# Two first weight pieces issued by ScalarE, and a last product that starts fresh in two PSUM banks, in an FNet and ReGLU mix on one core

## The chip, the cores and the metric

The kernel runs on 1 core of one Trainium2 chip. The metric is the device time of one execution in microseconds. The kernel before ran three times: 781.6, 779.49 and 779.66 us, median 779.66. One further execution was profiled; every row shown below from the kernel before is from it.

## The reference

```python
def a_ref(x, seq_re, seq_im, hid_re, hid_im):
    a = einsum("bsd,ed->bse", x, hid_re)
    b = einsum("bsd,ed->bse", x, hid_im)
    return einsum("ts,bse->bte", seq_re, a) - einsum("ts,bse->bte", seq_im, b)

def b_ref(x, W_gate, W_up, W_down):
    gate = einsum("bsd,df->bsf", x, W_gate)
    up   = einsum("bsd,df->bsf", x, W_up)
    gate = gate * (gate > 0)
    return einsum("bsf,fd->bsd", gate * up, W_down)

g = sigmoid((x * gate_w).sum(-1, keepdims=True))
out = g * a_ref(x, ...) + (1 - g) * b_ref(x, ...)
```

`x` is 1 x 2048 x 512 in fp32, the hidden size of the second branch is 1792, the matrices of the first are the cosines and sines of a Fourier transform over the hidden and the sequence dimension.

## The kernel before

**How the work is tiled.** Every matrix product is cut into 2 x 2 blocks and done as seven block products on sums of blocks (m = 1 to 7) instead of eight. Each fp32 operand is split in two parts that TensorE takes: `hi`, a rounded copy made by a ScalarE `copy` (CAST in the profile), and `lo`, what is left, made by a VectorE subtraction. One tile product is then three matmuls, left lo with right hi, left hi with right lo, left hi with right hi (`PARTS`, L365). A step of 128 x 512 outputs is one matmul row of the profile; a matmul on 256 columns is half of one.

**What sets the order.** No engine call is issued where it stands in the code. `op(key, f)` records a step, `pe(n, f)` records n matmuls and moves the clock of keys on, and `Plan.order` (L191) walks through all steps with a cost model (a matmul, a landing of a DMA, an issue per queue) and picks, for VectorE, ScalarE, SyncE and GpSimd, which step comes next; TensorE keeps the order of the code. `Step.run` (L122 to L126) then issues everything, so that all rows of the profile carry line L126, and names of tiles tell them apart. The order on each engine is fixed when the program is built: an engine that waits for one step holds all that stand behind it.

**Queues.** `load` (L356) is a DMA issued by SyncE (SP), which loads and writes most plain tiles. `store` and `accumulate` are issued by GpSimd. Before the change ScalarE issues no DMA.

**The start.** `warm_up` (L1230) sets `gs` to zero on VectorE and puts 18 matmuls of 256 columns on a constant into PSUM while the first loads are on their way. The first block product, m = 1, is done for two weight blocks, `ws[0]` and `ws[1]` (called w0 and w1 below; their raw tiles are `wr0`, two halves n of the columns and two halves k of the contraction each). TensorE's order is six matmuls on w0 with k half 0, six on w0 with k half 1, six and six on w1, then 24 matmuls of m = 2 (which need `x21`, the tile `x021`, and the column halves n = 1 of w0 and w1), then m = 5 and so on. `x11` (tile `x011`) comes in two halves, w0 in two quarters n = 0, k = 0 and k = 1, and the rest in larger pieces (L1254 to L1263). ScalarE casts each piece, VectorE takes the rest of it.

**The end.** `Joint` (L1067) is the last of the Fourier rounds: for y in `ORDER_Z` = (1, 5, 6, 3, 7, 2, 4), m in (0, 1) and hh in (0, 1) it records `product` (L1156), six matmuls each with left sides `self.w` and a right side `jc` that `right` (L1138) loads, casts on ScalarE (`jch`) and completes on VectorE (`jcl`). `evac` (L1167) combines the PSUM banks into the outputs `jo0` and `jo1`: with `last=True` it multiplies by the gate (`gg`), adds what the output already held (`jv0`, `jv1`) and writes by SP. `lead` gives how many keys ahead of their product the loads and the splits are planned. In the last call (L1388) the order is rearranged so that both products of y = 2 and y = 4 for m = 0 stand ahead of those for m = 1, and both products of y = 4, m = 1 are done in two column halves: ScalarE copies the second half of the bank of y = 4 into another bank, so that the first half can be finished and evacuated while the second is multiplied. The accumulations go on from m = 0 in those banks.

**The stage ahead of the end.** A `Shorter` round writes its outputs as `z`: VectorE adds two PSUM banks and a copy, then multiplies by the gate. Its last right sides are `cl`.

Of the kernel before, what the change touches and what calls it, by code (L numbers as in the profile page):

```python
# [14 lines left out]
P = 128  # L15
# [113 lines left out]
class Plan:  # L129
# [3 lines left out]

    MATMUL, WAIT, LANDING, COLD = 0.22667, 0.035, 2.5, 2.3

    ISSUE = {"sync": 0.5, "scalar": 0.5, "gpsimd": 0.9}

    REST = 60
# [52 lines left out]
    def order(self):  # L191
# [12 lines left out]
        while any(todo.values()):  # L204
            best = None
            for e, queue in todo.items():
                found = None
                near = queue[:1] if e == "tensor" or not queue else [*queue[:48], min(queue, key=turn.get)]
                for s in near:
                    if any(x.start is None for x in s.after):  # L210
                        continue
                    t = max(free[e], now)
                    for x in s.after:
                        t = max(t, x.end + (0 if x.engine == e else self.WAIT + 0.16 * (x.engine == "tensor")))
                    if e != "tensor":
                        t = max(t, (s.key - self.AHEAD[e]) * self.MATMUL + late)
                    new = {r.base for r in (*s.writes, *s.reads) if r.base.kind == "unit" and r.base not in begun}
                    if new:
                        short = live + bisect_left(ahead, turn[s]) + len(new) - UNITS
                        if short > 0:  # L220
                            if len(ends) < short:
                                continue
                            t = max(t, ends[short - 1])
                    if found is None or t < found[0] - 0.12:
                        found = t, s, new
                if found and (best is None or found[0] < best[0]):
                    best = found
            if best is None:
                raise ValueError(f"no way on at {len(done)}: {[(e, q[0].key, q[0].name) for e, q in todo.items() if q]}")
            t, s, new = best  # L230
            now = t
            while ends and ends[0] <= t:
                ends.pop(0)
                live -= 1
            live += len(new)
            for b in new:
                ahead.remove(min(turn[x] for x in b.uses))
            begun |= new
            todo[s.engine].remove(s)
            s.start = t  # L240
            if s.name == "dma_start":
                free[s.engine] = t + self.ISSUE[s.engine]
                line = max(line, free[s.engine]) + s.work * (self.COLD if 2.3 < t < 2.9 else 1)
                s.end = line + self.LANDING + (2.0 if "accum_op" in s.k else 0)
            else:
                s.end, free[s.engine] = t + s.work, t + s.hold
            if s.engine == "tensor" and s.key >= 0:
                late = max(late, t - s.key * self.MATMUL - 6 * self.MATMUL)
            for b in {r.base for r in (*s.writes, *s.reads) if r.base.kind == "unit"}:
                left[b] -= 1  # L250
                if not left[b]:
                    ends.append(max(x.end for x in b.uses))
                    ends.sort()
            done.append(s)
# [24 lines left out]
def kernel(ctx: ExitStack, tc, xP, xG, wgu, wd, cr, ci, wri, gw, out):  # L279
# [36 lines left out]

    gs = Buf(plan, "gs", [2, 32], kind="fixed", tile=small.tile([P, 2, 32], F32, name="gs"))

    gx = Buf(plan, "gx", [2, 32], kind="fixed", tile=small.tile([P, 2, 32], F32, name="gx"))

    def buf(name, shape=(2, N), dtype=F32):
# [80 lines left out]
    class Weights:  # L402
# [7 lines left out]
            self.d = buf("wd", [2, 2, 2, P], F32R)  # L410
            self.b = [[buf(f"wb{h}{x}", [2, 2, 2, P], F32R) for x in "hl"] for h in range(2)]

        def load(self, h, n=slice(0, 2), k=slice(0, 2)):
            load(self.raw[h][:, n, k], wgu[self.c, h, :, n, k])

        def a_hi(self, n=slice(0, 2), k=slice(0, 2)):
            E().scalar.copy(self.a[0][:, n, k], self.raw[0][:, n, k])
# [649 lines left out]
    class Joint:  # L1067
# [5 lines left out]
        def __init__(self, ms, banks, x=2, raw=None, last=False, lead=(0, 0), own=()):  # L1073
# [9 lines left out]
                op(base - 40, lambda: load(self.v[0].all, od[x - 2, :, 0:2]))  # L1083
                op(base + 20, lambda: load(self.v[1].all, od[x, :, 1]))
            order = [(y, m) for y in ORDER_Z for m in ms]
            if last:
                order[-4:] = [(y, m) for m in ms for y in ORDER_Z[-2:]]
            for n, (y, m) in enumerate(order):
                for hh in range(2):
                    self.right(m, y, hh, base + 12 * n + 6 * hh, made.get((m, hh)))  # L1090
            for y, m in order:
                for hh in range(2):
                    pe(6, self.product, m, y, hh)
                if m == ms[-1]:
                    self.evac(y, plan.now)
                elif last and y == 4:
                    op(plan.now, lambda: E().scalar.copy(self.half(1), self.bank(4, HALVES[1])))

        def lefts(self, m, base, raw, wide):
            if raw is None:  # L1100
# [37 lines left out]
        def right(self, m, x, hh, key, made):  # L1138
# [5 lines left out]

            if not made:
                op(key - self.READ - self.lead[0], read)
            op(key - self.HI - self.lead[1], lambda: E().scalar.copy(hi.all, raw.all))
            op(key - self.LO - self.lead[1], lambda: E().vector.tensor_sub(lo.all, raw.all, f32(hi.all)))

        def bank(self, x, cols=slice(0, N)):  # L1150
            return ps8[:, PAIRS[self.banks[BANK[x] in "yt"]].n + (BANK[x] in "mt"), cols]

        def half(self, n):
            return ps8[:, PAIRS["y"].n, HALVES[1]] if n else self.bank(4, HALVES[0])

        def product(self, m, x, hh):  # L1156
            l, c = self.w[m, x], self.c[m, x, hh]
            begin, end = m == self.ms[0] and hh == 0, m == self.ms[-1] and hh == 1
            halves = self.v and x == 4 and m == self.ms[-1]
            for cols in HALVES if halves else (slice(0, N),):  # L1160
                ps = self.half(HALVES.index(cols)) if halves else self.bank(x)
                for i in range(2):
                    for n, (a, b) in enumerate(PARTS):
                        mm(ps, l[a][:, 2 * hh + i], c[b][:, i, cols], start=x in FIRST and begin and i == n == 0,
                           stop=x not in (1, 5, 6, 7) and end and i == 1 and n == 2)

        def evac(self, x, key):  # L1167
            X, Y, M, T = (self.bank(k) for k in (1, 6, 5, 4))
# [25 lines left out]
            elif v:  # L1194
                for n, cols in enumerate(HALVES):
                    out, t = o[0][:, 1, cols], self.half(n)
                    op(key, lambda out=out, t=t, cols=cols: e.vector.tensor_mul(out, t, g[:, 0, cols]))
                    op(key, lambda out=out, cols=cols: combine(out, out, v[0][:, 1, cols], 1))
                    op(key, lambda out=out, cols=cols: load(od[self.x - 2, :, 1, cols], out))
            else:  # L1200
                op(key, lambda: e.vector.tensor_mul(o[0][:, 1], T, g[:, 0]))
# [27 lines left out]

    def warm_up():  # L1230
        E().vector.memset(gs.all, 0.0)
        for n in range(WARM):
            half = slice(n % 2 * (N // 2), (n % 2 + 1) * (N // 2))
            mm(ps8[:, (2, 3, 6, 7)[n // 2 % 4], half], ones[:, :P], ones, start=n in (0, 2, 4, 6), stop=True)
# [19 lines left out]
    for k in halves:  # L1254
        op(-99, x_load(0, "11", k))
        op(-99, ws[0].load, 0, halves[0], k)
    op(-99, ws[1].load, 0, halves[0])
    op(-99, x_load(0, "21"))
    for w in ws:
        op(-99, w.load, 0, halves[1])  # L1260
    op(-98, x_load(0, "12"))
    for w in ws:
        op(-98, w.load, 1)  # L1263
# [121 lines left out]
    Shorter(lb, 1, 1)  # L1385
    opened.resume(plan.now - 10)
    Shorter(lb, 1, 0)
    Joint((0, 1), "xm", last=True, lead=(80, 30))  # L1388

    plan.run(nc, unit)  # L1390

# [51 lines left out]
```

## Time and profile before

| what | us |
| --- | --- |
| median of three runs | 779.66 |
| the profiled execution | 779.72 |
| its span, first to last instruction | 777.9 |
| VectorE busy (736 instructions) | 665.5 |
| ScalarE busy (499 instructions) | 425.9 |
| GpSimd busy (178 instructions) | 121.5 |

The profiled execution lies 0.06 us above the median, and 1.82 us of it lie outside the span. The rows give an engine's time, the instructions of one kind, and in brackets what an engine waited for before them. PEld are TensorE's weight loads, which run beside its matmuls; a bracket on a PEld row is a wait of TensorE. SPq is the issuing of a DMA on SyncE's queue.

### The profile page before, as it was taken

The page shows a single profiled execution, that of the slowest core. Times are in us where ns is not written, and L with a number is a line of the kernel's source. Part 1 is how long each engine was busy: PE and PEld are TensorE (multiplying, and loading weights), DVE is VectorE, ACT ScalarE, POOL GpSimd, SP SyncE. Part 2 cuts the span into 40 slices and gives each one's busy share as a digit, 9 for nine tenths or more (in the row PEclk, how much of TensorE's full clock was granted, in tenths as well). Part 3 has the DMA queues.
Part 4 walks back from the last instruction along what each step waited for, and adds up shares of the span by engine and source line. Part 5 has one row for each costly group of instructions (what it writes and reads, how often), then busy time and mean ns, then how long its engine had stood idle before and what let it go on. Part 6 is the DMA issues. An engine that isn't in the chain of part 4 may idle for free.

```text
span 777.9 us, 9558 instructions
## 1 busy us (share of the span) xinstructions
PE 772.3 (99%) x3414; PEld 638.3 (82%) x3414; DVE 665.5 (86%) x736; ACT 425.9 (55%) x499; POOL 121.5 (16%) x178
## 2 busy tenths in 40 slices
PE   9999999999999999999999999999999999999997
PEld 7888888888888888888888888888888888888886
DVE  6999766766778685999996999998699899699898
ACT  6666444434455443566653667547644755345791
POOL 0021333332222332211000000030002011001000
PEclk9999999999999999999999999999999999999999
DMA  9246497999897999775369789989989997999982
GB/s 324 82 150 163 162 267 227 314 300 251 229 322 281 337 408 405 276 279 187 94 208 380 267 262 389 373 172 266 310 294 206 356 306 167 284 250 305 388 278 55
DMA packets 60255, 205.65 MB, mean 264 GB/s; under 512 B 7152, under 2 KB 7664, under 8 KB 60208
## 3 DMA queue, kind: packets, MB, share of 16 engines
q1 hardware_dynamic: 37264, 122.72, 43.5%
q0 software_dynamic: 22944, 82.32, 39.2%
q8 instruction: 27, 0.44, 0.2%
q14 instruction: 20, 0.16, 0.1%
HBM read 155.45 MB, written 74.73 MB: 296 GB/s over the span
## 4 chain that ended last, share of the span: by engine, by line
PE 98%; DMA 1%; SPq 0%; ACT 0%; DVE 0%; issue 0%; DVEq 0%
PE ps L126 98%; DMA x<-xP 1%; SPq L126 0%; DVE jo L126 0%; ACT xh L126 0%; ACT wah L126 0%; DVEq L126 0%
## 5 line engine op out<-in xcount | busy, mean ns | idle before, releaser
L126 PE MATMUL ps<-ch,ll 128*128 128x512 f32 x516 | 200.7, 389 | 0.0
L126 PE MATMUL ps<-cl,lh 128*128 128x512 f32 x516 | 200.7, 389 | 0.0
L126 PE MATMUL ps<-ch,lh 128*128 128x512 f32 x516 | 200.7, 389 | 0.0
L126 ACT CAST ch<-r 128x1024 fp32r<-128x1024 f32 x80 | 82.1, 1054 | 74.1 <-DVE r L126 64.6
L126 PEld LDWEIGHTS ps<-ch,ll 128*128 128x128 f32 x516 | 96.9, 188 | 20.1
L126 PEld LDWEIGHTS ps<-cl,lh 128*128 128x128 f32 x516 | 96.9, 188 | 20.1
L126 PEld LDWEIGHTS ps<-ch,lh 128*128 128x128 f32 x516 | 96.9, 188 | 20.0
L126 DVE TENSOR_TENSOR cl<-r,ch 128x1024 fp32r<-128x1024 f32 x80 | 95.6, 1221 | 7.7 <-ACT ch L126 6.1
L126 ACT CAST ch<-hr 128x1024 fp32r<-128x1024 f32 (+1 forms) x56 | 51.8, 945 | 43.5 <-DVE hr L126 21.2
L126 DVE TENSOR_TENSOR jcl<-jc,jch 128x1024 fp32r<-128x1024 f32 x56 | 65.6, 1222 | 7.8 <-issue 3.9
L126 ACT COPY s<-ps 128x1024 f32<-128x1024 f32 (+1 forms) x52 | 46.0, 884 | 47.6 <-PE ps L126 46.3
L126 ACT CAST jch<-jc 128x1024 fp32r<-128x1024 f32 x56 | 56.2, 1052 | 16.1 <-PE ps L126 14.0
L126 DVE TENSOR_TENSOR cl<-hr,ch 128x1024 fp32r<-128x1024 f32 (+1 forms) x56 | 60.1, 1087 | 5.1 <-ACT lh L126 2.7
L126 ACT ACTIVATE ps<-ps 128x512 f32<-128x512 f32 (+1 forms) x42 | 33.0, 785 | 55.0 <-PE ps L126 52.6
L126 POOL DMA_DIRECT2D out<-z x20 | 14.6, 729 | 297.3 <-DVE z L126 290.0
L126 DVE TENSOR_TENSOR r<-r,r 128x1024 f32<-128x1024 f32 x48 | 57.6, 1220 | 0.2
L126 DVE TENSOR_TENSOR u<-ps,s 128x1024 f32<-128x1024 f32 x28 | 34.1, 1221 | 13.4 <-PE ps L126 8.8
L126 POOL DMA_DIRECT2D hd<-h x35 | 23.0, 662 | 136.9 <-DVE h L126 125.6
L126 PE MATMUL ps<-xh,wb0l 128*128 128x512 f32 x112 | 43.8, 391 | 0.0
L126 PE MATMUL ps<-xh,wb0h 128*128 128x512 f32 x112 | 43.6, 389 | 0.0
L126 PE MATMUL ps<-xl,wb0h 128*128 128x512 f32 x112 | 43.6, 389 | 0.0
L126 PE MATMUL ps<-xh,wb1l 128*128 128x512 f32 x112 | 43.6, 389 | 0.0
(161 smaller groups left out, 1536.1 us busy)
## 6 DMA issues: line engine op xcount, KB each, us to landing
hr<-hd SPq DMA_DIRECT2D x33, 512.0 KB, 5.1
jc<-td SPq DMA_DIRECT2D x32, 512.0 KB, 8.1
td<-ci POOLq DMA_DIRECT2D x24, 512.0 KB, 10.1
r<-cr SPq DMA_DIRECT2D x24, 512.0 KB, 9.5
r<-ci SPq DMA_DIRECT2D x24, 512.0 KB, 8.5
out<-z POOLq DMA_DIRECT2D x20, 512.0 KB, 7.2
l<-ad SPq DMA_DIRECT2D x18, 512.0 KB, 8.7
wr<-wgu SPq DMA_DIRECT2D x16, 512.0 KB, 8.3
```

Source lines behind the costliest of these rows:

```text
L126: getattr(getattr(nc, self.engine), self.name)(*map(ap, self.a), **{k: ap(x) for k, x in self.k.items()})
```

## The change

At the start, the first piece of w1 (both k halves of its columns n = 0) and the second piece of w0 (its columns n = 1) are issued by ScalarE's queue, and no longer by SP's. A copy of `gs` into a new small tile `first` is put on ScalarE ahead of them, and the planner holds a DMA of ScalarE until 1.4 in its own time. At the end, the rearranged order is dropped; only the very last product (y = 4, last m, hh = 1) is in column halves; each half starts fresh in a bank of its own; its right side is multiplied by the gate beforehand; a new step `rest` multiplies what the bank of y = 4 holds by the gate and adds `jv0`; and the evacuation of a half is one addition. The lead of the last call changes from (80, 30) to (70, 44).

```diff
+    TABLE = 1.4
 ...
+                    if e == "scalar" and s.name == "dma_start":
+                        t = max(t, self.TABLE)
 ...
+    first = Buf(plan, "first", [32], kind="fixed", tile=small.tile([P, 32], F32, name="first"))
 ...
-        def load(self, h, n=slice(0, 2), k=slice(0, 2)):
-            load(self.raw[h][:, n, k], wgu[self.c, h, :, n, k])
+        def load(self, h, n=slice(0, 2), k=slice(0, 2), queue=None):
+            (queue or load)(self.raw[h][:, n, k], wgu[self.c, h, :, n, k])
 ...
-            if last:
-                order[-4:] = [(y, m) for m in ms for y in ORDER_Z[-2:]]
 ...
                 for hh in range(2):
+                    if self.fresh(m, y, hh):
+                        op(plan.now, self.rest)
                     pe(6, self.product, m, y, hh)
                 if m == ms[-1]:
                     self.evac(y, plan.now)
-                elif last and y == 4:
-                    op(plan.now, lambda: E().scalar.copy(self.half(1), self.bank(4, HALVES[1])))
 ...
+            if self.fresh(m, x, hh):
+                op(key - self.HI - self.lead[1] - 8, lambda: E().vector.tensor_mul(raw.all, raw.all, self.gate(0).to_broadcast([P, 2, N])))
 ...
+        def fresh(self, m, x, hh):
+            return self.v is not None and x == 4 and m == self.ms[-1] and hh == 1
+
         def half(self, n):
-            return ps8[:, PAIRS["y"].n, HALVES[1]] if n else self.bank(4, HALVES[0])
+            return ps8[:, PAIRS["y"].n + n, HALVES[n]]
 ...
-            halves = self.v and x == 4 and m == self.ms[-1]
+            halves = self.fresh(m, x, hh)
 ...
-                        mm(ps, l[a][:, 2 * hh + i], c[b][:, i, cols], start=x in FIRST and begin and i == n == 0,
+                        mm(ps, l[a][:, 2 * hh + i], c[b][:, i, cols], start=(x in FIRST and begin or halves) and i == n == 0,
 ...
+        def rest(self):
+            out = self.o[0][:, 1]
+            E().vector.tensor_mul(out, self.bank(4), self.g[:, 0])
+            combine(out, out, self.v[0][:, 1], 1)
 ...
-                    op(key, lambda out=out, t=t, cols=cols: e.vector.tensor_mul(out, t, g[:, 0, cols]))
-                    op(key, lambda out=out, cols=cols: combine(out, out, v[0][:, 1, cols], 1))
+                    op(key, lambda out=out, t=t: combine(out, out, t, 1))
 ...
         E().vector.memset(gs.all, 0.0)
+        E().scalar.copy(first[:], gs[:, 0])
 ...
-    op(-99, ws[1].load, 0, halves[0])
+    op(-99, ws[1].load, 0, halves[0], whole, plan.scalar.dma_start)
     op(-99, x_load(0, "21"))
-    for w in ws:
-        op(-99, w.load, 0, halves[1])
+    op(-99, ws[0].load, 0, halves[1], whole, plan.scalar.dma_start)
+    op(-99, ws[1].load, 0, halves[1])
 ...
-    Joint((0, 1), "xm", last=True, lead=(80, 30))
+    Joint((0, 1), "xm", last=True, lead=(70, 44))
```

The order of the instructions moves at three places. The first is ScalarE's at the start of the program; `wr0_84` is w0's raw tile before the change and `wr0_101` is w1's. Before:

```order
L126 ACT_TABLE_LOAD
L126 CAST wah_109<-wr0_84 128x256 x2
L126 CAST wah_131<-wr0_101 128x256 x2
L126 COPY ps_75<-ps_75 128x1024
L126 CAST xh2_155<-x021_103 128x512 x2
L126 CAST wah_109<-wr0_84 128x512
L126 COPY ps_75<-ps_75 128x1024
L126 CAST wah_131<-wr0_101 128x512
```

Now, where `wr0_86` is w0's and `wr0_95` w1's:

```order
L126 ACT_TABLE_LOAD
L126 COPY first_74<-gs_73 128x32
L126 DMA wr0_95<-wgu 128x512
L126 DMA wr0_86<-wgu 128x512
L126 CAST wah_115<-wr0_86 128x256
L126 CAST wah_131<-wr0_95 128x256
L126 CAST wah_115<-wr0_86 128x256
L126 CAST wah_131<-wr0_95 128x256
L126 CAST wah_115<-wr0_86 128x512
L126 COPY ps_76<-ps_76 128x1024
L126 CAST xh2_156<-x021_106 128x512 x2
L126 CAST wah_131<-wr0_95 128x512
```

Besides the copy and the two DMAs, the first cast of w1 now stands ahead of the second cast of w0, and the cast of w0's columns n = 1 and the copy of the bank ahead of the casts of `x21`. VectorE's subtractions of the same pieces change places in the same way. On SP the two pieces are gone: `x21` is now the fifth DMA and w1's second piece the sixth, where they were the sixth and the eighth.

The second place is VectorE's order around the last but one `z` before the end. Before:

```order
L126 TENSOR_TENSOR jll_5796<-js5_5691,jlh_5777 128x1024
L126 TENSOR_TENSOR jcl_5818<-jc_5624,jch_5790 128x1024
L126 TENSOR_TENSOR cl4_5828<-r11_5375,ch4_5807 128x1024
L126 TENSOR_TENSOR jcl_5843<-jc_5636,jch_5824 128x1024
L126 TENSOR_TENSOR z12_5855<-ps_75,s6_5679 128x1024
L126 TENSOR_TENSOR z12_5855<-z12_5855,gg_5510 128x1024
L126 TENSOR_TENSOR jll_5874<-js5_5716,jlh_5813 128x1024
L126 TENSOR_TENSOR jcl_5882<-jc_5648,jch_5841 128x1024
L126 TENSOR_TENSOR cl4_5893<-r11_5404,ch4_5859 128x1024
```

Now:

```order
L126 TENSOR_TENSOR jcl_5810<-jc_5654,jch_5796 128x1024
L126 TENSOR_TENSOR jll_5821<-js5_5716,jlh_5781 128x1024
L126 TENSOR_TENSOR jcl_5830<-jc_5664,jch_5813 128x1024
L126 TENSOR_TENSOR cl4_5848<-r11_5377,ch4_5824 128x1024
L126 TENSOR_TENSOR z12_5860<-ps_76,s6_5675 128x1024
L126 TENSOR_TENSOR z12_5860<-z12_5860,gg_5513 128x1024
L126 TENSOR_TENSOR jcl_5879<-jc_5680,jch_5832 128x1024
L126 TENSOR_TENSOR jll_5887<-js6_5692,jlh_5840 128x1024
L126 TENSOR_TENSOR jcl_5898<-jc_5694,jch_5866 128x1024
L126 TENSOR_TENSOR cl4_5910<-r11_5406,ch4_5875 128x1024
```

Two steps of the last call, one `jll` and one `jcl`, have moved from behind this `z` to ahead of it, and three steps instead of two stand between its gating and `cl4`, the last right side of the round.

The third place is the end of VectorE's order. Before:

```order
L126 TENSOR_TENSOR jcl_6208<-jc_5982,jch_6180 128x1024
L126 TENSOR_TENSOR jo1_6192<-ps_75,js_6052 128x512
L126 TENSOR_TENSOR jo1_6192<-jo1_6192,gg_5990 128x512
L126 TENSOR_TENSOR jo1_6192<-jo1_6192,jv1_6012 128x512
L126 TENSOR_TENSOR jo0_6231<-ps_75,gg_5990 128x512
L126 TENSOR_TENSOR jo0_6231<-jo0_6231,jv0_5870 128x512
L126 TENSOR_TENSOR jo0_6231<-ps_75,gg_5990 128x256
L126 TENSOR_TENSOR jo0_6231<-jo0_6231,jv0_5870 128x256
L126 TENSOR_TENSOR jo0_6231<-ps_75,gg_5990 128x256
L126 TENSOR_TENSOR jo0_6231<-jo0_6231,jv0_5870 128x256
```

Now:

```order
L126 TENSOR_TENSOR jc_6018<-jc_6018,gg_6007 128x1024
L126 TENSOR_TENSOR jo1_6172<-ps_76,js_6072 128x512
L126 TENSOR_TENSOR jo1_6172<-jo1_6172,gg_6007 128x512
L126 TENSOR_TENSOR jcl_6213<-jc_6018,jch_6203 128x1024
L126 TENSOR_TENSOR jo1_6172<-jo1_6172,jv1_6025 128x512
L126 TENSOR_TENSOR jo0_6224<-ps_76,gg_6007 128x512
L126 TENSOR_TENSOR jo0_6224<-jo0_6224,jv0_5892 128x512
L126 TENSOR_TENSOR jo0_6224<-ps_76,gg_6007 128x512
L126 TENSOR_TENSOR jo0_6224<-jo0_6224,jv0_5892 128x512
L126 TENSOR_TENSOR jo0_6224<-jo0_6224,ps_76 128x256 x2
```

The gating of the last right side is new; the gating and adding of y = 4 are now one pair of 512 columns ahead of the last product; behind the last product one addition for each half is left. On TensorE, twelve of the 24 matmuls of 256 columns became six of 512. ScalarE's copy of the bank's second half is gone.

## The prediction

> **What bounds the kernel now.** I read the head of the page first, then the chain of waits in order of time.
>
> ```profile
> span 777.9 us, 9558 instructions
> ...
> 3.07 6.43 DMA x<-xP
> ...
> 11.23 761.70 PE ps L126 x3366
> ...
> 774.28 0.42 DVE jo L126
> ```
>
> TensorE (PE) owns 761.70 of 777.9 us in one unbroken piece: 3366 matmuls at 761.70 / 3366 = 0.2263 us each. Nothing that moves on VectorE (DVE), ScalarE (ACT) or the queues inside that piece can help; it can only hurt by making PE wait. What can be won lies at the two ends: ahead of 11.23, where the chain goes through the landing of `x21`, and behind the last matmul. The profiled execution took 779.72 us, 0.06 above the median of 779.66, and all sums below are made against 779.72. A difference under 0.3% (2.34 us) is about what a measurement of this kernel can tell from no change.
>
> **The start as it is.** The timeline of SP's queue, ACT and PE, each with start, duration and in brackets what it waited for:
>
> ```profile
> 0.74 0.38 SPq L126 DMA_DIRECT2D x<-xP  x1
> ...
> 2.12 0.91 SPq L126 DMA_DIRECT2D wr<-wgu  x2
> ...
> 0.74 1.28 ACT L126 ACT_TABLE_LOAD   x1 [0.74 <-PEq L1436]
> ...
> 5.50 0.41 ACT L126 CAST wah<-wr 128x256 fp32r<-128x256 f32 x1 [0.84 <-DMA wr<-wgu]
> ...
> 7.94 1.00 ACT L126 COPY ps<-ps 128x1024 f32<-128x1024 f32 x1
> 9.52 1.14 ACT L126 CAST xh<-x 128x512 fp32r<-128x512 f32 x2 [0.58 <-DMA x<-xP]
> 10.57 0.61 ACT L126 CAST wah<-wr 128x512 fp32r<-128x512 f32 x1
> ...
> 0.78 4.00 PE L126 MATMUL ps<-const-bfloat16-1.0 128*128 128x256 bf16 x18 [0.78 <-PEq L1436]
> ...
> 6.13 0.41 PEld L126 LDWEIGHTS ps<-xh,wah 128*128 128x128 f32 x2
> ...
> 11.23 0.30 PEld L126 LDWEIGHTS ps<-xh,wah 128*128 128x128 f32 x2 [0.96 <-ACT wah L126]
> ```
>
> PE starts w0's second k half at 6.13 without a wait, finishes both weight blocks of m = 1 and then stands until 11.23 for m = 2, whose last cast ACT can only make once `x21` has landed at 9.5. How full the DMA engines are in these microseconds shows in the table by windows; its last two columns are their busy share and the GB/s moved. Below it are the landings (microseconds from issue) of w1's first piece and, as a median, of the two halves of `x11`:
>
> ```profile
> 1.00:2.00 1.00, 1.00 (x6) 0.69 (x5) 0.00 (x0) 1.00 (x1) 0.00 (x0) 1.00 0.16 33
> 2.00:3.00 1.00, 1.00 (x7) 0.72 (x5) 0.00 (x0) 0.02 (x1) 0.00 (x0) 1.00 0.91 313
> 3.00:4.00 1.00, 1.00 (x7) 0.67 (x6) 0.59 (x2) 0.00 (x0) 0.00 (x0) 1.00 0.95 252
> 4.00:5.00 1.00, 1.00 (x5) 0.53 (x4) 0.85 (x2) 0.41 (x1) 0.00 (x0) 1.00 0.99 317
> 5.00:6.00 1.00, 1.00 (x5) 0.82 (x5) 0.92 (x3) 0.41 (x1) 0.00 (x0) 1.00 1.30 257
> 6.00:7.00 1.00, 1.00 (x6) 0.82 (x5) 0.65 (x2) 0.00 (x0) 0.00 (x0) 1.00 0.70 219
> 7.00:8.00 1.00, 1.00 (x5) 0.69 (x5) 0.32 (x1) 0.76 (x3) 0.00 (x0) 1.00 0.82 205
> 8.00:9.00 1.00, 1.00 (x6) 0.80 (x5) 0.44 (x2) 0.94 (x1) 0.00 (x0) 1.00 0.97 383
> ```
> ```profile
> wr<-wgu SPq DMA_DIRECT2D x1, 256.0 KB, 4.6
> ...
> x<-xP SPq DMA_DIRECT2D x2, 256.0 KB, 3.0
> ```
>
> From 2.0 on the engines are 0.7 or more busy: the start is short of transfer, not of issuing. By 4.0 some 33 + 313 + 252 = 598 thousand bytes have moved, by 5.0 915, by 6.0 1172, by 7.0 1391, by 8.0 1596, by 9.0 1979. SP's order (in thousand bytes) is `x11` first half 262, w0's first quarter 131, `x11` second half 262, w0's second quarter 131 (786 together), w1's first piece 262 (1049), `x21` 524 (1573). So w0's second quarter had its last byte at 4.59 and landed at 5.5, when its cast starts, 0.9 later; w1's piece, issued at 2.59 (the second of the two from 2.12), had it at 5.52 and landed 4.6 after its issue, at 7.2, 1.67 later; `x21` at 7.89, landed at 9.5, 1.6 later.
>
> **The change at the start.** ACT's table load ends at 0.74 + 1.28 = 2.02. The copy into `first`, 32 columns, costs about 0.23: the casts are 0.41 for 256 and 0.61 for 512 columns, so 0.20 for each 256 on a fixed 0.21. ACT's first DMA then starts at 2.25 and takes 0.43 like SP's; SP's first ended its issue at 1.12, and 33 thousand bytes by 2.0 at 313 a microsecond means first bytes near 1.9, 0.8 later. ACT's bytes thus start near 3.5, when 472 have moved. From there w1's piece runs beside SP's, which has 314 to go until w0's second quarter is complete. I take equal shares, the middle between "all SP first" and "all ACT first". Then w1 has its last byte after 472 + 524 = 996, at 5.3, and lands by 7.0; w0's second quarter after 472 + 628 = 1100, at 5.72 instead of 4.59, and lands between 6.65 and 7.39 with the two lags; I take 7.39, the lag of the piece nearest to it in time. ACT casts w1's first half to 7.4, then w0's second quarter from 7.43 to 7.84: PE's second k half starts at 7.89 instead of 6.13 and PE stands 1.76 us. Then 18 matmuls of m = 1 at 0.2263 take 4.07, and m = 2 starts at 11.96. Is the rest there by then? w0's columns n = 1 follow w1 on ACT's queue, at 1520 thousand bytes, 7.6, landed by 9.2; their cast (0.61) ends at 9.85, the copy of the bank (1.00) at 10.85, the two casts of `x21` (landed at 10.2 after 1835 thousand bytes) at 11.99. It is, just. The old wait of 0.96 for `x21` swallows most of the new one: **+0.73** (11.96 against 11.23).
>
> The ends: if the queues took turns so that SP's bytes went first, w1 would land near 10, and since w0's cast now stands behind w1's on ACT, PE's second k half would start at 10, m = 2 at 14.1: +2.85. If ACT's went first from 3.5, w0's quarter has its last byte at 6.6 and lands at 8.2, m = 2 at 12.7: +1.5. If there is no collision, the price turns negative (rival 1).
>
> [...]
>
> What a later start gives back: two waits of PE behind it.
>
> ```profile
> 24.67 0.19 PEld L126 LDWEIGHTS ps<-xh,wb0h 128*128 128x128 f32 x1
> 25.19 0.19 PEld L126 LDWEIGHTS ps<-xh,wb0l 128*128 128x128 f32 x1 [0.34 <-DVE wb0l L126]
> ...
> 25.53 0.19 PEld L126 LDWEIGHTS ps<-xh,wb0h 128*128 128x128 f32 x1
> ```
>
> Three steps take 0.86 here instead of 3 x 0.2263 = 0.68: 0.18 lost to `wb0l`, whose pieces come by transfers that SP now issues two places earlier. With PE 0.73 later the wait is gone: **-0.18** (0 if DVE slips as far).
>
> **The order ahead of the end.**
>
> ```profile
> 721.67 1.23 DVE L126 TENSOR_TENSOR cl<-r,ch 128x1024 fp32r<-128x1024 f32 x1 [1.27 <-PE ps L126]
> 724.17 1.22 DVE L126 TENSOR_TENSOR jcl<-jc,jch 128x1024 fp32r<-128x1024 f32 x1 [1.27 <-PE ps L126]
> 725.62 1.23 DVE L126 TENSOR_TENSOR z<-ps,s 128x1024 f32<-128x1024 f32 x1 [0.22 <-ACT s L126]
> 726.88 1.23 DVE L126 TENSOR_TENSOR z<-z,gg 128x1024 f32<-128x1024 f32 x1
> ...
> 730.42 1.22 DVE L126 TENSOR_TENSOR cl<-r,ch 128x1024 fp32r<-128x1024 f32 x1
> ...
> 732.75 0.39 PE L126 MATMUL ps<-cl,lh 128*128 128x512 f32 x1
> ```
>
> DVE had 1.27 + 1.27 + 0.22 = 2.76 us idle ahead of `z`, and none from 725.62 until the very end. The new order puts two steps of about 1.2 into that idle time, which pays for the new gating (1.13 more work) with some 1.1 to spare. But between the gating of `z` and `cl` three steps of 1.2 stand instead of two: `cl` ends at 732.8 to 732.9 instead of 731.64, and PE wants it at 732.75. The cover of 1.1 us is gone there: 0 to +0.2, **+0.10** taken.
>
> **The end.**
>
> ```profile
> 770.61 0.28 PE L126 MATMUL ps<-jch,jwl 128*128 128x256 f32 x1
> ...
> 773.36 0.28 PE L126 MATMUL ps<-jch,jwh 128*128 128x256 f32 x1
> ...
> 771.24 0.68 DVE L126 TENSOR_TENSOR jo<-ps,gg 128x512 f32<-128x512 f32 x1
> 771.96 0.69 DVE L126 TENSOR_TENSOR jo<-jo,jv 128x512 f32<-128x512 f32 x1
> 773.03 0.42 DVE L126 TENSOR_TENSOR jo<-ps,gg 128x256 f32<-128x256 f32 x1 [0.38 <-PE ps L126]
> 773.49 0.43 DVE L126 TENSOR_TENSOR jo<-jo,jv 128x256 f32<-128x256 f32 x1
> 773.83 0.42 DVE L126 TENSOR_TENSOR jo<-ps,gg 128x256 f32<-128x256 f32 x1
> ```
>
> The 24 half matmuls go at (773.36 - 770.61) / 23 = 0.1196; twelve of them, 1.435, become six whole ones, 1.358: **-0.08**. Call the issue of the last whole matmul T. The last half of the first column half was issued 6 x 0.1196 = 0.72 before 773.36, at 772.64, and DVE answered at 773.03, 0.39 later; a whole matmul lasts 0.39 instead of 0.28, so `rest` starts at T + 0.50. Its product and sum take 0.72 (771.24 to 771.96) and 0.69: T + 1.91. The addition of the first half starts at 1.94, that of the second one step of 0.34 (773.49 to 773.83) later at 2.28, and ends with 0.42 at T + 2.70. PE's last half matmul is issued at T + 0.2263 + 11 x 0.1196 = T + 1.54, so DVE ends 1.16 behind it; before it was 774.28 + 0.42 - 773.36 = 1.34. **-0.18**. The bound is DVE's `rest`, not PE: if `rest` were free the end would be 0.39 + 0.42 behind the last matmul, another -0.35. If DVE can't use the idle time ahead of `z` it comes to `rest` 1.54 late, and the tail costs +1.36 (rival 4). The output's last transfer behind it keeps its size, and ACT's copy that goes was off the chain.
>
> **The sum**: +0.73 - 0.18 + 0.10 - 0.08 - 0.18 = +0.39, so 779.72 + 0.4 = **780.1**.
>
> **The rivals.**
>
> 1. No collision. Each piece lands as its row says from its issue: w1 at 2.25 + 3.0 = 5.25, w0's quarter at 5.5 as before. PE's second k half starts at 6.1 to 6.6, and `x21`, issued a place earlier, lets m = 2 start near 10.6: -0.63. With the rest that is -0.63 + 0.10 - 0.08 - 0.18 = -0.8, 778.9 (778.7 to 779.4); a part goes back to the waits for `wb0l`. For it: 383 GB/s from 8 to 9. Against it: shares of 0.91 to 1.30 at only 252 to 317 GB/s while w0's quarter is under way.
>
> [...]
>
> 3. ACT issues while its table is loading, near 1.0, since the issue is its sequencer's. The first bytes share with `x11` and w0's first quarter, PE's first k half is 0.7 late as well, the sum +1.3 to +1.7: 781.2. Against it: the copy into `first` stands between.
>
> 4. DVE is the bound at the end: +0.4 + 1.36 + 0.18 gives 781.7. Against it: the 2.76 us of idle time.
>
> **How the numbers follow.** Forecast 0.5 (its own range 779.6 to 780.8), rival 1 0.2 (778.7 to 779.4), rival 2 0.15, rival 3 0.08, rival 4 and SP's bytes first (779.72 + 2.5 = 782.2) 0.07 together. The range reaches from 778.9, inside rival 1, to 782.3, into rival 2. Faster by over 0.3% would need 777.3; all that PE could save at both ends is under 1.5, so 0.03. Slower by over 0.3% (782.1) holds the upper half of rival 2 and SP first, 0.15. The same: 0.82.
>
> **What would show it.** Right: ACT's first DMA near 2.3; a wait of PE ahead of w0's second k half that ends near 7.9; m = 2 near 12.0; no wait for `wb0l` at 25; a small wait for `cl` near 733; DVE's end 1.16 behind the last matmul, with no idle time between `rest` and the last two additions. Wrong: w0's second quarter cast at 5.5 as before (rival 1), ACT's DMA behind 3 us and a second k half behind 9 (rival 2), a first k half later than 4.7 (rival 3), DVE not waiting for PE ahead of `rest` (rival 4), or any wait of PE between 13 and 770 over 0.3 us.

## The result, and the profile after

The changed kernel takes 781.26 us (median of 20 runs, 780.95 to 783.85) against 779.57 for the kernel before (20 runs): 1.69 us more, ratio 1.0024, 95% interval 1.0018 to 1.003. It is a loss below the 0.3% that the prediction calls no change, inside its range, and 1.2 above its 780.1. Of it 1.3 lies inside the span (first to last instruction: a median of 779.1 in these 20 executions, 777.8 in those of the kernel before that were recorded with a span) and 0.36 outside it (2.16 against 1.80). The profiled execution took 782.25, 1.0 above the median, so a second one was taken (`after_again`, 780.77).

The start first. Two rows of TensorE before the change, then timelines of ScalarE and TensorE in the first profiled execution of the changed kernel (start, duration, in brackets the wait ahead):

```profile
4.71 0.88 PE L126 MATMUL ps<-xh,wah 128*128 128x512 f32 x2
...
7.28 0.62 PE L126 MATMUL ps<-xh,wal 128*128 128x512 f32 x2
```
```profile
0.73 1.28 ACT L126 ACT_TABLE_LOAD   x1 [0.73 <-PEq L1450]
0.97 0.86 ACTq L126 DMA_DIRECT2D wr<-wgu  x2
2.03 0.22 ACT L126 COPY first<-gs 128x32 f32<-128x32 f32 x1
5.23 0.71 ACT L126 CAST wah<-wr 128x256 fp32r<-128x256 f32 x2 [2.99 <-DMA wr<-wgu]
7.45 1.23 ACT L126 CAST wah<-wr 128x256 fp32r<-128x256 f32 x3 [1.50 <-DMA wr<-wgu]
...
5.69 1.22 PE L126 MATMUL ps<-xh,wah 128*128 128x512 f32 x2 [0.92 <-ACT wah L126]
6.71 1.06 PE L126 MATMUL ps<-xl,wah 128*128 128x512 f32 x2
...
10.07 0.62 PE L126 MATMUL ps<-xh,wal 128*128 128x512 f32 x2
10.53 0.62 PE L126 MATMUL ps<-xh,wah 128*128 128x512 f32 x2
...
13.27 0.62 PE L126 MATMUL ps<-xh,wah 128*128 128x512 f32 x2
```

ScalarE's two DMAs are issued at 0.97, while its table is still loading and a microsecond ahead of the copy that stands before them in its order. The first product starts at 5.69 instead of 4.71, with a break of 0.92 behind the warm-up, and its first ten matmuls take 10.07 - 5.69 = 4.38, 0.44 each, where those of before took 7.28 - 4.71 = 2.57, 0.26 each. m = 2 starts at 13.27 instead of 11.23.

The same engine in the second execution, `after_again`:

```profile
5.12 0.73 PE L126 MATMUL ps<-xh,wah 128*128 128x512 f32 x2 [0.35 <-ACT wah L126]
...
7.39 0.73 PE L126 MATMUL ps<-xh,wah 128*128 128x512 f32 x2 [0.60 <-ACT wah L126]
...
11.79 0.62 PE L126 MATMUL ps<-xh,wah 128*128 128x512 f32 x2
```

Here the break is 0.35, no matmul is slow, w0's second k half waits until 7.39 and m = 2 starts at 11.79.

What ScalarE's queue takes from SP's shows in the changed kernel's transfers from 3.0 to 3.5 and from 3.5 to 4.0 us, by queue (packets, MB, share of the engines; q1 is SP's, q10 ScalarE's), and in the landings of w0's two quarters, issued at 1.18 and 2.12:

```profile
q10 hardware_dynamic: 84, 0.16, 91.1%
q1 hardware_dynamic: 14, 0.01, 8.1%
...
q1 hardware_dynamic: 111, 0.10, 63.5%
q10 hardware_dynamic: 45, 0.07, 45.2%
...
wr<-wgu SPq DMA_DIRECT2D x1, 128.0 KB, 4.0
...
wr<-wgu SPq DMA_DIRECT2D x1, 128.0 KB, 5.3
```

In the first half microsecond SP's queue stands nearly still, in the second it has more than half of the packets. From 2.5 to 5.0 us together SP's queue moved 0.24 MB and ScalarE's 0.50, where SP's alone had moved 0.73 before. The first quarter lands at 5.2 (4.2 before), the second at 7.4 (5.5 before). Other pieces land earlier: w1's first at 0.97 + 3.3 = 4.3 (7.2 before), `x21` at 2.59 + 6.1 = 8.7 (9.5 before).

Ahead of the end, timelines of VectorE and of TensorE's weight loads in the changed kernel:

```profile
727.33 1.22 DVE L126 TENSOR_TENSOR z<-ps,s 128x1024 f32<-128x1024 f32 x1 [0.22 <-ACT s L126]
728.59 1.22 DVE L126 TENSOR_TENSOR z<-z,gg 128x1024 f32<-128x1024 f32 x1
729.73 1.22 DVE L126 TENSOR_TENSOR jcl<-jc,jch 128x1024 fp32r<-128x1024 f32 x1
730.98 1.23 DVE L126 TENSOR_TENSOR jll<-js,jlh 128x1024 fp32r<-128x1024 f32 x1
732.12 1.22 DVE L126 TENSOR_TENSOR jcl<-jc,jch 128x1024 fp32r<-128x1024 f32 x1
733.43 1.23 DVE L126 TENSOR_TENSOR cl<-r,ch 128x1024 fp32r<-128x1024 f32 x1
...
734.71 0.19 PEld L126 LDWEIGHTS ps<-cl,lh 128*128 128x128 f32 x1 [0.51 <-DVE cl L126]
```

`z` stands 1.71 behind its time of before, as TensorE does; three steps follow, `cl` ends at 734.66 and TensorE waits for it. At the end, timelines of TensorE, VectorE and SP:

```profile
775.39 0.28 PE L126 MATMUL ps<-jch,jwh 128*128 128x256 f32 x1
...
775.80 0.75 DVE L126 TENSOR_TENSOR jo<-jo,ps 128x256 f32<-128x256 f32 x2
...
776.25 0.33 SPq L126 DMA_DIRECT2D out<-jo  x1
...
776.68 0.38 SPq L126 DMA_DIRECT2D out<-jo  x1
```

The same two issues of SP before the change:

```profile
773.94 0.33 SPq L126 DMA_DIRECT2D out<-jo  x1
...
774.73 0.33 SPq L126 DMA_DIRECT2D out<-jo  x1
```

The traces give the spans as 780.08 and, before, 777.95. VectorE ends 775.80 + 0.75 = 776.55, which is 1.16 behind the last matmul (1.34 before), but the span ends 4.69 behind it (777.95 - 773.36 = 4.59 before).

With the distance of equal matmuls of the two kernels as a ruler, the difference can be followed along TensorE (us against the profiled execution of before):

| execution | at 38.9 (m = 4) | behind the last `cl` | last matmul | span | time |
| --- | --- | --- | --- | --- | --- |
| changed, first | +1.71 | +2.11 | +2.03 | +2.13 | +2.53 |
| changed, second | +0.22 | +0.66 | +0.58 | +0.67 | +1.05 |
| start_only | +0.92 | +0.92 | +0.92 | +0.92 | +1.05 |
| end_only | +0.10 | +0.50 | +0.42 | +0.52 | +0.51 |

From m = 4 to the last `Shorter` round nothing moves by more than 0.04 in any of them (the second execution stands at +0.26 there). The start differs from execution to execution; `cl` costs 0.40, the matmuls at the end give 0.08, and what stands behind the last matmul costs 0.09 or 0.10 wherever the new end is in.

### The profile page after: what moved, and what is told of

Same layout as the page of the kernel before. It is cut to its first block, busy times and chain, and to the rows that moved or that the text cites. A ratio compares the mean times of both kernels' runs of the same rounds, so it can differ in the third digit from the quotient of the medians.

```text
span 780.1 us, 9535 instructions
## 1 busy us (share of the span) xinstructions
PE 773.9 (99%) x3408; PEld 639.6 (82%) x3408; DVE 666.9 (85%) x737; ACT 425.0 (54%) x499; POOL 121.2 (16%) x178
```

## The experiments

**The two halves of the change.** `start_only` is the kernel before with the lines of the diff on `TABLE`, `first`, `load(queue=...)` and the two loads; `end_only` is the changed kernel in which nothing uses them:

```diff
-    op(-99, ws[1].load, 0, halves[0], whole, plan.scalar.dma_start)
+    op(-99, ws[1].load, 0, halves[0])
     op(-99, x_load(0, "21"))
-    op(-99, ws[0].load, 0, halves[1], whole, plan.scalar.dma_start)
-    op(-99, ws[1].load, 0, halves[1])
+    for w in ws:
+        op(-99, w.load, 0, halves[1])
 ...
-        E().scalar.copy(first[:], gs[:, 0])
```

> The kernel before with the start of the change alone (ScalarE's two pieces, the copy into first, the planner's 1.4). Theory A: the cost lies at the start. ScalarE issues its DMAs near 1.0, w0's first quarter lands 0.9 later, TensorE stands about 0.9 us after the warm-up and then runs some ten matmuls at 0.43 instead of 0.23; m = 2 starts near 13.3 instead of 11.2, some 0.3 is given back by the waits for wb0l: 781.0 to 781.5. Theory B: the start costs only the shared transfer, +0.4, and the rest is lost ahead of the end by the order on VectorE: 780.0.

> The end of the change alone, with the start of before. Theory A: a wait for cl of about 0.4 ahead of the end and a gain of 0.1 at the tail: 779.6 to 780.0, a difference from before of +0.1 to +0.4. Theory B: 780.8 or more.

Measured: `start_only` 780.69 against 779.62 (ratio 1.0013, 1.0004 to 1.0022), `end_only` 780.16 against 779.62 (1.001, 1.0001 to 1.0019). Their differences, 1.07 and 0.54, add up to 1.61, near the change's 1.69. That they add up so well may be partly chance: inside the span the halves lose 1.0 and 0.6 (medians), the change 1.3; outside it 0.1 and nothing, the change 0.36. Both parts lose; the start somewhat less and the end more than theory A had said. TensorE in `start_only`:

```profile
5.17 0.75 PE L126 MATMUL ps<-xh,wah 128*128 128x512 f32 x2 [0.39 <-ACT wah L126]
...
8.30 0.73 PE L126 MATMUL ps<-xh,wah 128*128 128x512 f32 x2 [1.44 <-ACT wah L126]
```

No matmul is slow here, and the loss is the wait of 1.44 for w0's second quarter, as the prediction's sum had it (7.89), 0.4 later. Theory A's slow matmuls are not needed for this loss.

**ScalarE's DMAs held until the table is loaded.** The first copy writes 32 columns of w1's raw tile, which the DMA then overwrites, so the DMA must wait for the copy:

```diff
-        E().scalar.copy(first[:], gs[:, 0])
+        E().scalar.copy(ws[1].raw[0][:, 0, 0, 0, 0:32], gs[:, 0])
```

> The changed kernel, but the first copy of ScalarE writes 32 columns of w1's raw tile (overwritten by the DMA), so that the DMA waits for the copy and so for the table load. Theory A: ScalarE's DMA near 2.3; w0's first quarter lands at 4.3 and TensorE starts at 4.7 without a break; a wait ahead of w0's second k half until about 7.9; m = 2 near 12.0; 780.0 to 780.4, 1 us below the changed kernel. Rival: if the time of ScalarE's issue is not the cause, it stays at 781.2.

Measured: 782.25 against 779.62 (1.0034, 1.0022 to 1.0047), not below the changed kernel: theory A falls here. Timelines of ScalarE's queue and TensorE:

```profile
2.28 0.86 ACTq L126 DMA_DIRECT2D wr<-wgu  x2
...
5.50 1.22 PE L126 MATMUL ps<-xh,wah 128*128 128x512 f32 x2 [0.72 <-ACT wah L126]
6.52 1.05 PE L126 MATMUL ps<-xl,wah 128*128 128x512 f32 x2
```

The DMA is issued at 2.28, as the prediction had assumed (2.25), and yet w0's first quarter is late, and slow matmuls follow. Why that quarter is late with ScalarE's first bytes moving only from 4 us on is not explained; in the next run, with the same DMAs, it was on time. So the moment of the issue is not the cause.

**The order of ScalarE's casts.** In `held` w0's second quarter had landed before its cast, which stood behind w1's. `held_order` lets w1's cast follow it:

```diff
+        if w is ws[0]:
+            held.append(plan.steps[-1])
+        elif n == halves[0]:
+            plan.steps[-1].after.add(held[1])
```

> The run held, with the cast of w0's second quarter on ScalarE put back ahead of w1's first cast. Theory: in held w0's second quarter has landed at 6.0 (issue 2.12, landing 3.9) but its cast stands behind w1's, which lands at 7.9; so the cast moves from about 8.3 to about 6.1 and TensorE's wait ahead of the second k half goes. If the first products run slow as in held (first product at 5.5, ten at 0.43), m = 2 comes near 12.9 and the time is 781.0 to 781.9; at full pace near 11.5 and 780.2 to 780.6. Rival: the order of the casts does not matter, 782.2 as held.

Measured: 781.45 against 779.64 (1.0025, 1.0014 to 1.0035). TensorE:

```profile
4.76 0.73 PE L126 MATMUL ps<-xh,wah 128*128 128x512 f32 x2
...
7.65 0.73 PE L126 MATMUL ps<-xh,wah 128*128 128x512 f32 x2 [1.23 <-ACT wah L126]
...
11.88 0.62 PE L126 MATMUL ps<-xh,wah 128*128 128x512 f32 x2
```

This is the start that the prediction described (4.71, 7.89, 11.96), with nothing slow in it. The quarter's cast moved from 8.3 only to 7.2, since this time the quarter itself landed 5.0 after its issue instead of 3.9: whatever order the casts have, it is late. Sharing is a part of that at most: from 3.0 to 4.0, with no packet yet on ScalarE's queue, SP's moved 0.13 MB (0.07 and 0.06) where it had moved 0.25 before, and why is not known. At the last `cl` the kernel stands 1.46 behind before, of which 0.41 came with `cl`.

**Half the bytes on ScalarE's queue.** `one_piece` is `start_only` with w1's first piece back on SP:

```diff
-    op(-99, ws[1].load, 0, halves[0], whole, plan.scalar.dma_start)
+    op(-99, ws[1].load, 0, halves[0])
```

> The start of the change alone with one piece (256 KB, w0's columns n = 1) on ScalarE's queue instead of two; w1's first piece stays on SP behind w0's second quarter. Theory A (the bytes that ScalarE's queue moves early push w0's quarters back, byte for byte): half the delay of start_only, w0's second quarter cast near 6.6 instead of 5.5 (before) and 7.8 (start_only), TensorE's second k half near 7.0, m = 2 near 11.2 to 11.5: 779.6 to 780.0. Rival: a second queue as such costs, whatever it moves: 780.5 or more.

Measured: 779.98 against 779.64 (1.0004, 0.9995 to 1.0013), 0.7 below `start_only`. TensorE:

```profile
5.18 0.73 PE L126 MATMUL ps<-xh,wah 128*128 128x512 f32 x2 [0.52 <-ACT wah L126]
...
10.95 0.61 PE L126 MATMUL ps<-xh,wah 128*128 128x512 f32 x2
```

The wait ahead of the second k half is gone and m = 2 starts 0.28 ahead of before, without a wait. Over all its executions the median span is 777.8, that of before; in `start_only` it is 778.8. Inside the span the loss went by the bytes that overtake w0's quarters (none with 256 KB on ScalarE's queue, 1.0 with 512 KB), and there a second queue as such cost nothing. The rival falls for the span; the 0.34 that the time still loses, within its interval, lies outside it (see the table below).

**The slow matmuls.** Three runs ask whether they come from the break: `warm24` is the changed kernel with the first line below, `before_warm14` the kernel before with the second, and `after_again` the changed kernel once more, with no edit.

```diff
-    WARM = 18
+    WARM = 24
 ...
-    WARM = 18
+    WARM = 14
```

> The changed kernel with 24 warm-up matmuls instead of 18, so that TensorE has no break before the first product at 5.7. Theory A with the clock: the first product still starts near 5.7 but at 0.23 a matmul; w0's second k half near 7.9, m = 2 near 12.0: 780.0 to 780.3. Rival: if the slow matmuls come from late weights or a busy memory and not from the break, they stay at 0.43 and the time at 781.2.

> The kernel before with 14 warm-up matmuls instead of 18: a break of about 0.8 ahead of the first product at 4.7, with no transfer changed. If a break of that length alone brings the slow pace: some nine matmuls at 0.43 from 4.7 on, 1.8 lost, of which the old wait for x21 (0.7) takes some: 780.5 to 780.9 and a wide spread. Rival: the break costs nothing by itself: 779.6.

> The changed kernel once more, for a second profiled execution. Its first profiled execution took 782.25, 1.0 above the median of 781.26. Theory (the ten slow matmuls behind the break belong to that execution, not to the change): this one has its first product near 5.2 to 5.7 at 0.23 a matmul, the second k half at 7.9 to 8.4, m = 2 at 12.0 to 12.6, and takes 781.0 to 781.4. Rival (a break always brings the slow pace): ten matmuls at 0.43, m = 2 near 13.3 again.

Measured: `before_warm14` 780.64 against 779.66 (1.0011, 1.0003 to 1.002), inside what was expected. TensorE there, with no transfer changed:

```profile
4.62 1.22 PE L126 MATMUL ps<-xh,wah 128*128 128x512 f32 x2 [0.69 <-ACT wah L126]
5.64 1.05 PE L126 MATMUL ps<-xl,wah 128*128 128x512 f32 x2
...
9.05 0.76 PE L126 MATMUL ps<-xh,wal 128*128 128x512 f32 x2
9.65 0.62 PE L126 MATMUL ps<-xh,wah 128*128 128x512 f32 x2
```

The slow pace lasts until about 9 with no transfer changed: a break of 0.7 behind a shorter warm-up is enough for it. The break does not start it, though. The warm-up matmuls themselves run at the slow pace (4.00 / 18 = 0.222 for 256 columns in the kernel before, against 0.1196 at the end), and without a long break the first products can still be slow, as here in `end_only`, with the start of before:

```profile
4.69 1.22 PE L126 MATMUL ps<-xh,wah 128*128 128x512 f32 x2
5.71 0.81 PE L126 MATMUL ps<-xl,wah 128*128 128x512 f32 x2
```

Of the traces with the transfers of before and 18 warm-up matmuls, `before` is at full pace from 5.43, `end_cl` from 5.93, `end_only` from 6.35 and `end_cl_2q` from 6.72; behind breaks of 0.69 to 0.92 it is 9.65 (`before_warm14`), 9.66 (`held`) and 10.07 (the first profile of the changed kernel). So a break of that length goes with some 3 us more at the slow pace; whether the break or the four missing matmuls did it in `before_warm14` is not separated. `after_again` (781.4 against 779.66; 1.0027, 1.0016 to 1.0039) had a break of 0.35 in its profile and no slow matmul, so the change does not always bring it. `warm24` filled the break and its profile has the full pace from 6.71 on:

```profile
5.71 1.19 PE L126 MATMUL ps<-xh,wah 128*128 128x512 f32 x2
6.71 0.65 PE L126 MATMUL ps<-xl,wah 128*128 128x512 f32 x2
```

Its profiled execution took 781.05, 1.2 less than the first of the changed kernel, but its median is 781.83 (1.0027, 1.0017 to 1.0037), not the 780.0 to 780.3 expected. So a longer warm-up is no remedy. Its median span is 779.2, that of the changed kernel 779.1: the warm-up won nothing there in the median, and the rest of its loss lies outside the span. Only one execution of each run has a trace, so how often the slow matmuls come stays open; but 14 of the changed kernel's 20 spans lie from 778.8 to 779.3 and only four are as long as the first profiled one (780.1 or more), so the median loss is not that of so long an execution.

**The end.** `end_cl` is `end_only` with one number changed; `end_cl_2q` then lets ScalarE issue the last output:

```diff
-    Joint((0, 1), "xm", last=True, lead=(70, 44))
+    Joint((0, 1), "xm", last=True, lead=(70, 42))
 ...
-                    op(key, lambda out=out, cols=cols: load(od[self.x - 2, :, 1, cols], out))
+                    op(key, lambda out=out, cols=cols, n=n: (E().scalar.dma_start if n else load)(od[self.x - 2, :, 1, cols], out))
```

> The run end_only with the lead (70, 42) in place of (70, 44), which gives an order of VectorE with two steps instead of three between the gating of z and the last cl. Theory: the wait of TensorE for cl near 733 (0.35 lost) goes: 779.6 to 780.0, 0.2 to 0.4 below end_only. Rival: it comes back at another right side later: as end_only, 780.2.

> The run end_cl with the very last of the output's DMAs issued by ScalarE instead of SP. Theory: SP needs 0.43 for each of the two last issues, and the last addition ends 0.34 behind the one ahead, so the last issue was held back by about 0.1; from the last matmul to the end of the span 4.72 (end_only) goes to about 4.6: 0.1 less than end_cl. Rival: the two last transfers share the same engines and the second is no earlier: no difference, 4.7.

Measured: `end_cl` 779.87 against 779.64 (1.0002, 0.9993 to 1.0011), 0.3 below `end_only`, and in its trace TensorE waits nowhere ahead of the end: 0.18 behind before at m = 4 and 0.18 behind the last `cl`. The wait for `cl` is the order's, and it did not come back later. `end_cl_2q` 779.92 (1.0003, 0.9994 to 1.0012): no difference. Timelines of TensorE and ScalarE's queue there:

```profile
773.38 0.28 PE L126 MATMUL ps<-jch,jwh 128*128 128x256 f32 x1
...
774.57 0.38 ACTq L126 DMA_DIRECT2D out<-jo  x1
```

Its span is 778.06. The last issue is 1.19 behind the last matmul instead of 1.29, and the span still ends 778.06 - 773.38 = 4.68 behind it, as in `end_cl`. The rival holds: issuing the last output 0.10 sooner does not end the program sooner.

**A version that beats both?** `one_warm20` is `one_piece` with two more warm-up matmuls; `one_cl_warm20` adds the new end with the lead (70, 42).

```diff
-    WARM = 18
+    WARM = 20
```

> The run one_piece with 20 warm-up matmuls, which fill the 0.4 of TensorE's break ahead of its first product (5.18). In one_piece's profile m = 2 started at 10.95 without a wait and TensorE was 0.48 ahead of before from 225 us to the end, but its median was 0.3 above before. If the break is what costs it in the other executions: 779.1 to 779.4, below before. Rival: the break is harmless, as one_piece, 779.7 to 780.0.

> The run one_warm20 with the end of the change under the lead (70, 42). By the runs so far that end is worth -0.08 in the matmuls and +0.1 behind the last matmul: the same as one_warm20 within 0.2. Rival (the shorter tail on VectorE counts after all): 0.2 below one_warm20.

Measured: 779.82 (1.0002, 0.9994 to 1.0011) and 780.19 (1.0004, 0.9995 to 1.0012) against 779.66. In the traces TensorE's last matmul stands 0.69 and 0.56 ahead of before, but no median is below it. `one_cl_warm20`'s runs fall into two groups, five from 779.16 to 779.35 and six from 780.19 to 781.4; their spans are alike (777.4 to 777.6 and 777.4 to 778.1), and the groups part outside the span, with 1.74 to 1.82 and 2.49 to 4.00. Neither is faster in a way that was measured.

**Time outside the span.** Each execution was recorded with its time and its span (to a tenth), so the time outside the span can be read for all of them, traced or not:

| kernel | executions | median time | median span | outside, lowest to highest |
| --- | --- | --- | --- | --- |
| before | 29 | 779.66 | 777.8 | 1.72 to 1.93 |
| changed | 20 | 781.26 | 779.1 | 2.10 to 2.31 |
| start_only | 11 | 780.69 | 778.8 | 1.86 to 2.00 |
| end_only | 11 | 780.16 | 778.4 | 1.73 to 1.84 |
| one_piece | 11 | 779.98 | 777.8 | 2.10 to 2.25 |
| one_warm20 | 11 | 779.82 | 777.7 | 2.11 to 2.29 |
| one_cl_warm20 | 11 | 780.19 | 777.5 | 1.74 to 4.00 |
| warm24 | 9 | 781.83 | 779.2 | 2.13 to 3.26 |

The changed kernel's 0.36 there is in every execution, and no part of the change that ran alone explains it: in the median `start_only`, with both of ScalarE's DMAs, has 0.09 of it and `end_only` none, while `one_piece`, with one DMA of ScalarE, has nearly all. What it is was not tried.

## Why the prediction was right or wrong

The time lay in the range and the direction was that of the sum (+0.39), but the sum was 1.3 too small, and its own narrower range (779.6 to 780.8) did not hold the median. Of the 1.3, the end gives 0.6 (in the traces 0.40 - 0.08 + 0.10 = 0.42 lost instead of 0.16 gained), the time outside the span 0.36 and the start the rest (0.92 lost in the trace of `start_only` instead of 0.55). That the wider range held it is partly luck: it reached to 782.3 for a first DMA of ScalarE behind 3 us (rival 2). No run shows that term: the DMA came at 0.97 in the changed kernel and at 2.28 in `held`. Rival 3's sign came instead, a first k half later than 4.7; its 781.2 meets the median, but by luck too, since it put the whole loss at the start.

- **ScalarE's first DMA at 2.25: wrong.** It came at 0.97. The step that failed is "ACT's first DMA then starts at 2.25"; rival 3 had it right, and the argument against that rival (the copy into `first` stands between) was the error: the DMA row stands at 0.97 and the copy's at 2.03, so the issue waited here neither for the table load (0.73 to 2.01) nor for the copy ahead of it; it stands 0.04 behind the end of the setting of `gs` (0.82 + 0.11), which that copy reads. Yet `held` shows that putting this right would not have saved the time.
- **"PE's first k half" on time: wrong.** With two pieces on ScalarE's queue issued near 1.0 and 18 warm-up matmuls the first product started at 5.12, 5.17 and 5.69; with one piece at 5.04 to 5.24, with none at 4.69 to 5.00.
- **Equal shares: near over the whole stretch, wrong at each moment; the landing met by luck.** From 2.5 to 5.0 ScalarE's queue moved 0.50 to 0.52 MB and SP's 0.24 (first profile), 0.37 (`after_again`) and 0.40 (`start_only`). In packets the two were near even over those 2.5 us in two traces, 288 on ScalarE's queue to 279 and 291 on SP's (271 to 215 in the first profile); in half a microsecond they were not (84 to 14 from 3.0 to 3.5 in the first profile, then 45 to 111), and nothing here shows why. w0's second quarter landed at 7.4, the value taken, by two errors that cancel: SP's queue had moved the 786 thousand bytes up to its end at 6.5 (0.79 MB by then), not at 5.72, and the landing followed 0.9 later, not 1.67. In the other two traces it landed at 6.9 and 7.8.
- **PE's wait ahead of the second k half, m = 2 at 11.96 (+0.73): mechanism right, size spread.** m = 2 came at 11.79 (`after_again`), 11.88 (`held_order`), 12.49 (`start_only`) and 13.27 (the first profile of the changed kernel): +0.56 to +2.04. The slow pace that makes the last (0.44 a matmul) is in no term of the sum. TensorE had not yet left it when the warm-up ended, and in `before_warm14` a break of 0.7 behind 14 warm-up matmuls went with it until about 9. Two smaller things: the 6.13 against which the prediction set its 7.89 is a weight load, whose matmul started at 6.36, so TensorE was to stand 1.53 and not 1.76; and the 18 matmuls behind the wait took 4.19 to 4.40 in the first three of these traces instead of 4.07.
- **-0.18 from `wb0l`: right.** From m = 5 to m = 4 the changed kernel makes up 1.86 - 1.71 = 0.15 in one trace and 0.39 - 0.22 = 0.17 in the other.
- **`cl` +0.10: mechanism right, four times too small.** It is +0.40 to +0.42 in every trace that has the new end with this lead. `cl` starts 733.43 - 727.33 = 6.10 behind `z`, where the prediction had at most 6.06 (732.9 - 1.22 - 725.62). TensorE then takes up again 0.05 after VectorE's end, at 734.71, which is 0.25 behind 732.75 + 1.71, and loses another 0.15 on the steps behind the wait, which the sum had not counted.
- **-0.08 for the matmuls: right** (2.11 to 2.03, 0.50 to 0.42).
- **The tail, -0.18: right on VectorE, +0.1 at the end.** VectorE ended 1.16 behind the last matmul, to the hundredth. But from the last matmul to the end of the span the nine traces with the new end have 4.67 to 4.69, and of the five with the old one four have 4.58 or 4.59 and one 4.75. The step that failed is to count VectorE's end as the program's: behind it stand the last issue and transfer. SP issues the last two outputs 776.68 - 776.25 = 0.43 apart, so the last issue comes 1.29 behind the last matmul instead of 1.37, and its transfer then takes 2.0 us to land instead of 1.9. `end_cl_2q` shows that an earlier issue does not shorten this.
- **DVE not the bound ahead of the end: right** (rival 4 fell): it waited 0.85 for TensorE ahead of `rest`.
- **A term that no step had.** Outside the span the changed kernel takes 0.36 more (2.16 against 1.80, medians), in every execution. The prediction measured all its terms inside the span and kept the 1.82 outside it as a constant without a reason. The cause stays open.

## What to carry to other kernels

The second issuing queue brought forward here what it carried (w1's first piece from 7.2 to 4.3) and pushed back what it overtook (w0's second quarter from 5.5 to 7.4): put there what is needed last, and no more than the early pieces can spare. Cover that the planner gave away on one engine (one step more ahead of the last right side) cost the whole overshoot (0.25) and 0.15 more on TensorE's steps behind it. Before counting a saving behind the last matmul, see in another kernel of the same kind whether the end moves when the last issue does. Compare spans as well as times: a part of this loss, and all of `one_piece`'s, lies outside the span.

## What was not expected of the hardware

- A DMA on ScalarE's queue was issued at 0.97 with its table load running from 0.73 to 2.01 and a copy ahead of it in the order that ran at 2.03, 0.02 behind the load.
- TensorE's slow pace is not in the granted clock. This window of the first profile of the changed kernel lies among the slow matmuls, and its third column from the right, the granted clock, is 1.00:

```profile
8.00:9.00 1.00, 1.00 (x4) 0.81 (x3) 1.00 (x4) 0.68 (x2) 0.00 (x0) 1.00 1.07 428
```

- TensorE ran at the slow pace from its first matmul at 0.78, through the whole warm-up in most traces. Full pace came within the warm-up in `one_warm20`, whose 20 matmuls took 3.84 (18 took 4.00 in the kernel before, 0.222 each), and at 6.72, 5.9 us behind the first matmul, in `end_cl_2q`; with a break of 0.69 to 0.92 it came 8.9 to 9.3 us behind it. The slow pace is about half the full one (0.44 a matmul of 512 columns against 0.23); how long it lasts varies, from under 3.9 us to 9.3 us behind the first matmul. A break of 0.34 to 0.52 did not keep the slow pace in the five traces that have one (`after_again`, `start_only`, `one_piece`, `one_warm20`, `one_cl_warm20`).
- A DMA busy share near 1 is not one rate. From 2.5 to 5.0 us the kernel before moved 0.73 MB on one queue, at a share of 97.1%; `start_only` moved 0.92 MB on two (54.5% and 47.9%), with fewer small packets (192 of 579 under 2 KB, 310 of 543 before). The first profile of the changed kernel had two queues and 0.75 MB. What sets the rate was not tried; the prediction took the rates of before as they were.
